# Attention inputs loaded in 1 KB runs, transposed by VectorE straight into place, and a new order for the first units

## The chip, the cores and the metric

The kernel runs on one core of a Trainium2 chip. The metric is the device time of one execution in microseconds (us). A run at a lower TensorE clock, or over 1.5% above the fastest of the same kernel, is marked slow and is not used in ratios. Several chips were used (the medians of the kernel before were 301.31 to 302.19 us), so each experiment is compared with the kernel before, timed in the same rounds.

In this kernel TensorE (PE in the profile) multiplies matrices, ScalarE (ACT) computes exponentials and copies, VectorE (DVE) does element-wise work and 32x32 block transposes, GpSimd is POOL, and SyncE (SP) issues most transfers (DMA; 129 of 197 issues in the profile before). SBUF is the on-chip memory, PSUM holds the products of TensorE. KB is 1024 bytes.

## The reference

Windowed attention with 8 global keys and a linear bias per head, then a layer of 8 experts in which every expert takes exactly 384 tokens, chosen greedily in order of the logits:

```python
# q, k, v: [4, 8, 768, 64] float32 (batch, heads, positions, head dimension)
scores = q @ k.T / 8 - slope[head] * dist    # keep: local (96 back) or global (first 8)
a = softmax(where(keep, scores, -1e9))
x = (a @ v) as [3072 tokens, 512]
logits = x @ w_gate                          # [3072, 8]
# greedy: largest logit first, 384 tokens per expert, each token once
out[tokens of e] = relu(x[tokens of e] @ w1[e]) @ w2[e]
```

## The kernel before

The attention runs in 8 units, u = 0 to 7; a unit is 4 heads of one batch element. The matmuls of the scores take queries and keys with the head dimension on the partitions (32 x 128 and 32 x 215 in the trace), while they lie in memory with the position outside. So a unit's 4 heads of q (768 KB) are loaded with 32 partitions for each head and 24 consecutive positions (6 KB) in each partition; VectorE transposes blocks of 32 x 32, and ScalarE copies the result into the order that the matmuls want.

```python
NJ = S_ // 32                       # 24 positions in a partition
qr = natp.tile([128, NJ, D_], FP32)
kr = natp.tile([128, NJ, D_], FP32)     # one buffer each: the load of unit u+2's keys
...                                     # waits for the transposes of unit u+1's
def load_u(u, dst, src):                # ONE transfer of 128 partitions x 6 KB
    b, hf = divmod(u, 2)
    nc.sync.dma_start(dst.rearrange("p j d -> p (j d)"),
                      src[b, 4*hf : 4*hf+4].rearrange("a (c j) d -> (a c) (j d)", j=NJ))

def blocks(key, src, g):                # writes 32 neighbouring floats at a time
    t = ttp.tile([128, NJ, 32], FP32, tag="tT", name=f"tT_{key}_{g}")
    nc.vector.transpose(out=t, in_=src[:, :, 32*g : 32*g+32])
    tTs[key, g] = t

def qT_out(u, g):                       # ScalarE puts the positions in order
    ...
    nc.scalar.copy(out=qTs[u][:, g, :].rearrange("p (c j) -> p c j", j=NJ),
                   in_=tTs.pop((f"q{u}", g)).rearrange("p j c -> p c j"))
...                                     # kA_out: the same for keys, in three copies
```

The program is written by hand in the order in which each engine meets its work. A unit's loop body (scores are made for unit `u` while unit `u-1` is attended, that is, its softmax weights are multiplied with v):

```python
load_u(0, kr, k); load_u(0, qr, q)
... # transposes and copies of unit 0
load_u(1, kr, k); load_u(1, qr, q)
... # w_gate
for n in range(NB): load_v(n)           # values of pairs 0 to 3, 20 transfers in 256-byte pieces
for u in range(NU + 1):
    ps = scores(u, 0); expo(u, 0, ps)   # TensorE, then exponentials on ScalarE
    if u == 0: build_W(0..3)            # mask tiles, ScalarE
    ... # u > 0: kT(u+1) on VectorE, load_u(u+2, kr, k), then masks of group 0
    av(A); oT_out(A, 0); oT_out(A, 1)   # attend of the first head pair of u-1
    pr = sums(A)                        # row sums and logits into a PSUM buffer
    ... # kA_out(u+1), qT(u+1, 0), qT_out(u+1, 0)
    sums_out(A, pr)                     # VectorE frees pr (transpose LT<-pr)
    ps = scores(u, 1); expo(u, 1, ps)
    if u == 0: build_W(4..7)
    ... # qT(u+1, 1), load_u(u+2, qr, q), masks of group 1
    ... # tok(A): TensorE transposes into PSUM (pk); tok_out(A): VectorE reads it (x)
    av(Bp); ...                         # attend of the second head pair
    ps = scores(u, 2); expo(u, 2, ps); mask(2*u, 2)
    pr = sums(Bp); sums_out(Bp, pr); ...
...
fill(4)                                 # four dummy matmuls before the routing
```

`pr` and `pk` share two PSUM buffers, so TensorE waits when VectorE comes late to empty them (11.46 us in the profile after).

The softmax here doesn't subtract the row's maximum and nothing guards it: scores larger than these inputs give would overflow.

Of the kernel before, what the change touches and what calls it, by code (L numbers as in the profile page):

```python
# [9 lines left out]
FP32 = mybir.dt.float32  # L10
# [7 lines left out]
B_, H_, S_, D_ = 4, 8, 768, 64  # L18
# [24 lines left out]
def kernel(  # L43
# [159 lines left out]
    with ExitStack() as actx:  # L203
# [24 lines left out]
        ttp = actx.enter_context(tc.tile_pool(name="ttp", bufs=2))  # L228
# [11 lines left out]
        NJ = S_ // 32  # L240
        qr = natp.tile([128, NJ, D_], FP32)
        kr = natp.tile([128, NJ, D_], FP32)
        kAs = [natp.tile([128, 2, NT, 128], FP32, name=f"kA{i}") for i in range(2)]
        NC5 = KT // NJ
        v7s = [natp.tile([128, 2, NT, D_], FP32, name=f"v7_{i}") for i in range(NB)]
        qTs = {}
        tTs = {}
        LASTK = S_ - KT * (NT - 1)

        def load_u(u, dst, src):  # L250
            b, hf = divmod(u, 2)
            nc.sync.dma_start(dst.rearrange("p j d -> p (j d)"),
                              src[b, 4 * hf : 4 * hf + 4].rearrange("a (c j) d -> (a c) (j d)", j=NJ))

# [12 lines left out]
        def blocks(key, src, g):  # L267
            t = ttp.tile([128, NJ, 32], FP32, tag="tT", name=f"tT_{key}_{g}")
            nc.vector.transpose(out=t, in_=src[:, :, 32 * g : 32 * g + 32])  # L269
            tTs[key, g] = t  # L270

        def kT(u, g):
            blocks(f"k{u}", kr, g)

        def kA_out(u, g):
            t = tTs.pop((f"k{u}", g)).rearrange("p j c -> p c j")
            kA = kAs[u % 2][:, g]
            n6 = NT - 1
            nc.scalar.copy(out=kA[:, 0:n6, 8:128].rearrange("p i (c j) -> p i c j", j=NJ),  # L279
                           in_=t[:, 0 : n6 * NC5, :].rearrange("p (i c) j -> p i c j", c=NC5))  # L280
            nc.scalar.copy(out=kA[:, n6, 8 : 8 + LASTK].rearrange("p (c j) -> p c j", j=NJ),
                           in_=t[:, n6 * NC5 : 32, :])
            nc.scalar.copy(out=kA[:, :, 0:8],
                           in_=t[:, 0:1, 0:8].to_broadcast([128, NT, 8]))

        def qT(u, g):
            blocks(f"q{u}", qr, g)

        def qT_out(u, g):
            if g == 0:  # L290
                qTs[u] = ktp.tile([128, 2, S_], FP32, tag="qT", name=f"qT{u}")
            nc.scalar.copy(out=qTs[u][:, g, :].rearrange("p (c j) -> p c j", j=NJ),  # L292
                           in_=tTs.pop((f"q{u}", g)).rearrange("p j c -> p c j"))
# [158 lines left out]
        with tc.manual_schedule():  # L452
# [6 lines left out]
            for g in range(2):  # L459
                kT(0, g)  # L460
                kA_out(0, g)
            for g in range(2):
                qT(0, g)
                qT_out(0, g)
# [8 lines left out]
            for u in range(NU + 1):  # L473
                A, Bp = 2 * (u - 1), 2 * (u - 1) + 1
                cur, prev, nxt = u < NU, u > 0, u + 1 < NU
                if cur:
                    ps = scores(u, 0)
                    expo(u, 0, ps)
                    if u == 0:
                        for h in range(4):  # L480
                            build_W(h)

                def keys():
                    if nxt:
                        kT(u + 1, 0)
                        kT(u + 1, 1)
                        if u + 2 < NU:
                            load_u(u + 2, kr, k)

                def first_masks():  # L490
                    if cur:
                        mask(2 * u, 0)
                        mask(2 * u + 1, 0)

                if u == 0:
                    first_masks()
                    keys()
                else:
                    keys()
                    first_masks()  # L500
                if prev:
                    av(A)
# [485 lines left out]
```

## Time and profile before

| | before |
|---|---|
| time, median of 3 runs | 302.26 us (301.77 to 302.31) |
| the profiled run | 304.70 us, span 302.9 us, clock 0.977 |
| start, to the first attend | 0 to 36.5 us |
| units 2 to 6, from scores to scores | 16.24 to 16.45 us each |
| unit 2's scores start | 51.06 us |
| last transposes to first routing matmul | 157.43 to 163.24 us |

The profiled run was 2.4 us slower than the median of the timed ones (its clock fell to 0.57 at 200 to 204 us, at the start of the experts).

Busy times on the profile's page (us, share of the span, instructions), then the start and one unit in the windows view. The columns of a window are its limits and length, busy time and count of PE, PEld, DVE, ACT and POOL, the granted clock (1.00 is TensorE's full speed), the mean busy share of the DMA engines (above 1 in places, 1.05 at 12 to 30 us) and GB/s:

```profile
PE 261.4 (86%) x3174; PEld 180.1 (59%) x3174; DVE 156.4 (52%) x301; ACT 143.8 (47%) x225; POOL 81.2 (27%) x126
```

```profile
0.00:36.00 36.00, 15.41 (x142) 12.53 (x144) 14.93 (x22) 23.67 (x31) 9.18 (x34) 1.00 0.84 218
...
51.06:67.30 16.24, 16.21 (x309) 13.70 (x308) 13.02 (x21) 12.95 (x18) 0.00 (x0) 1.00 0.72 177
```

In the units TensorE is busy for 16.21 of 16.24 us, so only TensorE's own work or a new wait changes them. In the start it is busy for less than half (15.41 of 36 us).

TensorE in the start, in the timeline (start, length, what, and the idle time before with its releaser):

```profile
11.31 1.10 PE L317 MATMUL ps<-qT,kA 32*128 32x215 f32 x8 [11.31 <-ACT qT L292]
...
16.22 4.01 PE L317 MATMUL ps<-qT,kA 32*128 32x215 f32 x32 [0.97 <-ACT P L331]
27.18 4.42 PE L317 MATMUL ps<-qT,kA 32*128 32x215 f32 x48 [6.94 <-ACT P L331]
32.65 3.94 PE L317 MATMUL ps<-qT,kA 32*128 32x215 f32 x32 [1.06 <-ACT P L331]
36.53 2.52 PE L365 MATMUL po<-P,v 128*64 128x215 f32 x36
```

The gap of 6.94 us is an exponential that stands on ScalarE behind mask tiles and copies of unit 1. The groups of instructions that the change touches (count, busy us, mean ns; then idle time before them):

```profile
L269 DVE STREAM_TRANSPOSE tT_q<-qr 128x768 f32<-128x768 f32 x16 | 15.6, 977 | 7.8 <-ACT kA L283 7.8
L269 DVE STREAM_TRANSPOSE tT_k<-kr 128x768 f32<-128x768 f32 x16 | 14.7, 954 | 4.6 <-DMA kr<-in_k_dram 4.6
L279 ACT COPY kA<-tT_k 128x720 f32<-128x720 f32 x16 | 23.7, 1484 | 6.3 <-DVE tT_k L269 6.3
L292 ACT COPY qT<-tT_q 128x768 f32<-128x768 f32 x16 | 24.8, 1556 | 0.0
```

Unit 2's keys are the next thing needed after the start. Their load is issued at 30.00 us, and VectorE begins to transpose them almost without a wait:

```profile
30.00 1.56 SPq L252 DMA_DIRECT2D kr<-in_k_dram  x1
...
35.74 1.84 DVE L269 STREAM_TRANSPOSE tT_k<-kr 128x768 f32<-128x768 f32 x2 [1.08 <-DMA kr<-in_k_dram]
```

### The profile page before, as it was taken

The page shows a single profiled execution, that of the slowest core. Times are in us where ns is not written, and L with a number is a line of the kernel's source. Part 1 is how long each engine was busy: PE and PEld are TensorE (multiplying, and loading weights), DVE is VectorE, ACT ScalarE, POOL GpSimd, SP SyncE. Part 2 cuts the span into 40 slices and gives each one's busy share as a digit, 9 for nine tenths or more (in the row PEclk, how much of TensorE's full clock was granted, in tenths as well). Part 3 has the DMA queues.
Part 4 walks back from the last instruction along what each step waited for, and adds up shares of the span by engine and source line. Part 5 has one row for each costly group of instructions (what it writes and reads, how often), then busy time and mean ns, then how long its engine had stood idle before and what let it go on. Part 6 is the DMA issues. An engine that isn't in the chain of part 4 may idle for free. (4 is left out here: it accounts for less than half of the span.)

```text
span 302.9 us, 7456 instructions
## 1 busy us (share of the span) xinstructions
PE 261.4 (86%) x3174; PEld 180.1 (59%) x3174; DVE 156.4 (52%) x301; ACT 143.8 (47%) x225; POOL 81.2 (27%) x126
## 2 busy tenths in 40 slices
PE   0454899999999999999997888879999998999940
PEld 0343788888888788888874343345655554555510
DVE  3255558879797978685524756322233222233020
ACT  3679686978869595963310000013522522513500
POOL 5060000003069000000004000473765556551230
PEclk9999999999999999999997999979999999999995
DMA  5799665695999998222024996159999999530220
GB/s 208 222 194 209 226 174 150 181 199 87 291 153 285 235 255 224 61 58 54 5 52 77 212 210 110 35 117 206 221 212 254 233 267 265 209 111 32 102 108 5
DMA packets 52568, 49.27 MB, mean 163 GB/s; under 512 B 29744, under 2 KB 44080, under 8 KB 52528
## 3 DMA queue, kind: packets, MB, share of 16 engines
q0 software_dynamic: 15680, 26.22, 41.4%
q1 hardware_dynamic: 36848, 22.50, 28.1%
q8 instruction: 27, 0.44, 0.6%
q14 instruction: 13, 0.11, 0.1%
HBM read 56.05 MB, written 9.44 MB: 216 GB/s over the span
## 5 line engine op out<-in xcount | busy, mean ns | idle before, releaser
L317 PE MATMUL ps<-qT,kA 32*128 32x215 f32 (+2 forms) x896 | 54.2, 369 | 20.6 <-ACT qT L292 11.6
L928 ACT ACTIVATE hT<-ph 128x384 bf16<-128x384 f32 x64 | 31.4, 491 | 71.9 <-PE ph L925 71.3
L317 PEld LDWEIGHTS ps<-qT,kA 32*128 32x128 f32 x896 | 45.4, 207 | 27.2 <-ACT qT L292 12.2
L331 ACT ACTIVATE P<-ps 128x860 f32<-128x860 f32 (+1 forms) x48 | 41.0, 893 | 27.5 <-PE ps L317 26.8
L345 DVE TENSOR_TENSOR P<-P,Wm 128x860 f32<-128x860 f32 (+1 forms) x32 | 32.9, 1049 | 18.0 <-ACT P L331 10.5
L365 PE MATMUL po<-P,v 128*64 128x215 f32 (+6 forms) x576 | 40.4, 292 | 0.0
L365 PEld LDWEIGHTS po<-P,v 128*64 128x64 f32 x576 | 34.4, 136 | 7.6 <-issue 3.5
L894 POOL DMA_INDIRECT xe<-x_tok,idi x24 | 23.4, 974 | 36.4 <-DVE idi L748 28.2
L934 PE MATMUL po<-w_late,hT 128*128 128x512 bf16 x144 | 32.9, 379 | 0.0
L937 DVE COPY ot<-po 128x512 f32<-128x512 f32 x24 | 16.5, 692 | 30.7 <-PE po L934 24.2
L925 PE MATMUL ph<-xT,w_late 128*128 128x384 bf16 x192 | 32.2, 326 | 0.0
L938 POOL DMA_INDIRECT out_dram<-ot,idi x24 | 23.6, 982 | 31.7 <-DVE ot L937 28.5
L934 PEld LDWEIGHTS <-hT 128*128 128x128 bf16 x192 | 18.3, 98 | 19.5
L576 POOL DMA_DIRECT2D w_late<-in_moe_w_dram x12 | 10.4, 874 | 69.1 <-DVE x L437 62.6
L907 DVE COPY xT<-pxe 128x512 bf16<-128x512 bf16 x24 | 9.5, 422 | 37.4 <-PE pxe L906 36.4
L396 PE MATMUL pr<-P,onesx 128*32 128x192 f32 (+11 forms) x768 | 27.6, 259 | 0.0
L279 ACT COPY kA<-tT_k 128x720 f32<-128x720 f32 x16 | 23.7, 1484 | 6.3 <-DVE tT_k L269 6.3
L925 PEld LDWEIGHTS <-w_late 128*128 128x128 bf16 x192 | 18.8, 98 | 13.1
L396 PEld LDWEIGHTS pr<-P,onesx 128*32 128x32 f32 x768 | 24.7, 109 | 2.1
L292 ACT COPY qT<-tT_q 128x768 f32<-128x768 f32 x16 | 24.8, 1556 | 0.0
L617 PE MATMUL pw<-w_early,ident_bf 128*128 128x512 bf16 x51 | 19.8, 389 | 2.7 <-DVE x L437 0.6
L338 DVE TENSOR_TENSOR P<-P,Wm 128x860 f32<-128x860 f32 x16 | 16.3, 1064 | 10.2 <-ACT P L331 10.2
(139 smaller groups left out, 263.5 us busy)
## 6 DMA issues: line engine op xcount, KB each, us to landing
w_late<-in_moe_w_dram POOLq DMA_DIRECT2D x12, 1024.0 KB, 12.5
kr<-in_k_dram SPq DMA_DIRECT2D x8, 768.0 KB
qr<-in_q_dram SPq DMA_DIRECT2D x8, 768.0 KB
v<-in_v_dram SPq DMA_DIRECT2D x32, 180.0 KB
w_early<-in_moe_w_dram POOLq DMA_DIRECT2D x8, 512.0 KB, 8.9
x_tok<-x SPq DMA_DIRECT2D x32, 96.0 KB
v<-in_v_dram SPq DMA_DIRECT2D x32, 14.0 KB
v<-in_v_dram SPq DMA_DIRECT2D x16, 24.0 KB
```

The lines of the kernel that those rows point to most:

```text
L279: nc.scalar.copy(out=kA[:, 0:n6, 8:128].rearrange("p i (c j) -> p i c j", j=NJ), in_=t[:, 0 : n6 * NC5, :].rearrange("p (i c) j -> p i c j ...
L292: nc.scalar.copy(out=qTs[u][:, g, :].rearrange("p (c j) -> p c j", j=NJ), in_=tTs.pop((f"q{u}", g)).rearrange("p j c -> p c j"))
L317: nc.tensor.matmul(ps[a // 2][:, a % 2, o : o + w], lhsT=kA[r, gd, i, :], rhs=qTt[r, gd, KT * i : KT * i + w], start=(gd == 0), stop=(gd = ...
L331: nc.scalar.activation(P[:, :, 0 : GW[g]], ps[w_][:, :, 0 : GW[g]], AF.Exp, scale=0.125)
L345: nc.vector.tensor_tensor(out=P[:, :, 0 : GW[g]], in0=P[:, :, 0 : GW[g]], in1=Wm[:, h0 : h0 + 2, lo : lo + GW[g]], op=ALU.mult)
L365: nc.tensor.matmul(po[n][bk][64 * t : 64 * t + 64, a - QB * bk : z - QB * bk], lhsT=v7[:, t, i, :], rhs=P[:, t, o + a - q0 : o + z - q0], ...
L396: nc.tensor.matmul(o_, lhsT=l_, rhs=r_, start=first[gq], stop=True, skip_group_check=True)
L894: tc.keep_in_program_order(nc.gpsimd.indirect_dma_start(out=xe, out_offset=None, in_=x_tok[:, :], in_offset=bass.IndirectOffsetOnAxis(ap=i ...
L925: nc.tensor.matmul(ph, lhsT=w1_of(e)[:, kc, 128 * fc : 128 * fc + 128], rhs=xT_e[:, kc, :, :].rearrange("p t n -> p (t n)"), start=(kc == ...
L928: nc.scalar.activation(hT[:, fc, :], ph, AF.Relu)
L934: nc.tensor.matmul(po, lhsT=hT[:, fc, 128 * t : 128 * t + 128], rhs=w2_of(e)[:, fc, :], start=(fc == 0), stop=(fc == NFC - 1))
L938: s = nc.gpsimd.indirect_dma_start(out=out[:, :], out_offset=bass.IndirectOffsetOnAxis(ap=idi[:, TSLAB * e + t : TSLAB * e + t + 1], axis= ...
```

## The change

The change has three parts.

1. **Layout.** The positions go to partitions four at a time (`NS = 4`, 1 KB runs), so that the transpose can write q into its final place, and k in position order, with a stride of four floats. ScalarE's copies of q go away, and those of k become contiguous. Each load becomes four transfers of 32 partitions.
2. **Order.** Unit 0's three score groups follow each other; its masks come later, and unit 1's loads and transposes are spread between them.
3. The four dummy matmuls before the routing are dropped.

```diff
-        NJ = S_ // 32
-        qr = natp.tile([128, NJ, D_], FP32)        # kr alike
+        NS = 4
+        qr = natp.tile([128, NBLK, NS, D_], FP32)  # kr alike; NBLK = 6
+        kTn = natp.tile([128, 2, S_], FP32)
         def load_u(u, dst, src):
             b, hf = divmod(u, 2)
-            nc.sync.dma_start(dst.rearrange("p j d -> p (j d)"),
-                              src[b, 4 * hf : 4 * hf + 4].rearrange("a (c j) d -> (a c) (j d)", j=NJ))
+            for a in range(4):
+                nc.sync.dma_start(dst[32 * a : 32 * a + 32].rearrange("c j s d -> c j (s d)"),
+                                  src[b, 4 * hf + a].rearrange("(j c s) d -> c j (s d)", j=NBLK, s=NS))
+        def blocks(dst, src, g):
+            nc.vector.transpose(out=dst.rearrange("p (j c s) -> p j s c", j=NBLK, s=NS),
+                                in_=src[:, :, :, 32 * g : 32 * g + 32])
... # kT writes kTn; kA_out copies kTn in three contiguous pieces; qT writes qTs[u]; qT_out is gone
-            for u in range(NU + 1):                # u == 0 leaves the loop:
+            ps = scores(0, 0); expo(0, 0, ps)      # (one statement a line in the kernel)
+            build_W(0); build_W(1)
+            kT(1); load_u(2, kr, k); weight_piece()
+            ps = scores(0, 1); expo(0, 1, ps)
+            kA_out(1); mask(0, 0); qT(1); load_u(2, qr, q)
+            ps = scores(0, 2); expo(0, 2, ps)
+            build_W(2); build_W(3)
+            ... # the other masks of unit 0
+            for u in range(1, NU + 1):
...
-            fill(4)
```

More of the change, by code (lines that the diff above doesn't have):

```diff
@@ L227 @@
         ktp = actx.enter_context(tc.tile_pool(name="ktp", bufs=2))
-        ttp = actx.enter_context(tc.tile_pool(name="ttp", bufs=2))
         tp = actx.enter_context(tc.tile_pool(name="tp", bufs=3))
@@ L239 @@
         NB = 4
-        NJ = S_ // 32
-        qr = natp.tile([128, NJ, D_], FP32)
-        kr = natp.tile([128, NJ, D_], FP32)
+        NS = 4
+        qr = natp.tile([128, NBLK, NS, D_], FP32)
+        kr = natp.tile([128, NBLK, NS, D_], FP32)
+        kTn = natp.tile([128, 2, S_], FP32)
         kAs = [natp.tile([128, 2, NT, 128], FP32, name=f"kA{i}") for i in range(2)]
-        NC5 = KT // NJ
         v7s = [natp.tile([128, 2, NT, D_], FP32, name=f"v7_{i}") for i in range(NB)]
         qTs = {}
-        tTs = {}
         LASTK = S_ - KT * (NT - 1)
@@ L265, in load_v, with kT, kA_out, qT @@
                               v[b, h : h + 2, KT * (NT - 1) : S_].rearrange("t u d -> u t d"))
-        def blocks(key, src, g):
-            t = ttp.tile([128, NJ, 32], FP32, tag="tT", name=f"tT_{key}_{g}")
-            nc.vector.transpose(out=t, in_=src[:, :, 32 * g : 32 * g + 32])
-            tTs[key, g] = t
-        def kT(u, g):
-            blocks(f"k{u}", kr, g)
-        def kA_out(u, g):
-            t = tTs.pop((f"k{u}", g)).rearrange("p j c -> p c j")
-            kA = kAs[u % 2][:, g]
-            n6 = NT - 1
-            nc.scalar.copy(out=kA[:, 0:n6, 8:128].rearrange("p i (c j) -> p i c j", j=NJ),
-                           in_=t[:, 0 : n6 * NC5, :].rearrange("p (i c) j -> p i c j", c=NC5))
-            nc.scalar.copy(out=kA[:, n6, 8 : 8 + LASTK].rearrange("p (c j) -> p c j", j=NJ),
-                           in_=t[:, n6 * NC5 : 32, :])
-            nc.scalar.copy(out=kA[:, :, 0:8],
-                           in_=t[:, 0:1, 0:8].to_broadcast([128, NT, 8]))
-        def qT(u, g):
-            blocks(f"q{u}", qr, g)
-        def qT_out(u, g):
-            if g == 0:
-                qTs[u] = ktp.tile([128, 2, S_], FP32, tag="qT", name=f"qT{u}")
-            nc.scalar.copy(out=qTs[u][:, g, :].rearrange("p (c j) -> p c j", j=NJ),
-                           in_=tTs.pop((f"q{u}", g)).rearrange("p j c -> p c j"))
+        def blocks(dst, src, g):
+            nc.vector.transpose(out=dst.rearrange("p (j c s) -> p j s c", j=NBLK, s=NS),
+                                in_=src[:, :, :, 32 * g : 32 * g + 32])
+        def kT(u):
+            for g in range(2):
+                blocks(kTn[:, g, :], kr, g)
+        def kA_out(u):
+            n6 = NT - 1
+            kA = kAs[u % 2]
+            nc.scalar.copy(out=kA[:, :, 0:n6, 8:128], in_=kTn[:, :, 0 : n6 * KT].rearrange("p g (i k) -> p g i k", i=n6))
+            nc.scalar.copy(out=kA[:, :, n6, 8 : 8 + LASTK], in_=kTn[:, :, n6 * KT : S_])
+            nc.scalar.copy(out=kA[:, :, :, 0:8],
+                           in_=kTn[:, :, 0:8].rearrange("p g (o k) -> p g o k", o=1).to_broadcast([128, 2, NT, 8]))
+        def qT(u):
+            qTs[u] = ktp.tile([128, 2, S_], FP32, tag="qT", name=f"qT{u}")
+            for g in range(2):
+                blocks(qTs[u][:, g, :], qr, g)
         wpieces = []
@@ L458 @@
                 nc.vector.memset(v7s[i][:, :, NT - 1, :], 0.0)
-            for g in range(2):
-                kT(0, g)
-                kA_out(0, g)
-            for g in range(2):
-                qT(0, g)
-                qT_out(0, g)
+            kT(0)
+            kA_out(0)
+            qT(0)
             load_u(1, kr, k)
@@ L472 @@
                                         in0=wg_sb[64 * t : 64 * t + 64], scalar1=LSCALE, scalar2=None, op0=ALU.mult)
-            for u in range(NU + 1):
+            ps = scores(0, 0)
+            expo(0, 0, ps)
+            build_W(0)
+            build_W(1)
+            kT(1)
+            load_u(2, kr, k)
+            weight_piece()
+            ps = scores(0, 1)
+            expo(0, 1, ps)
+            kA_out(1)
+            mask(0, 0)
+            qT(1)
+            load_u(2, qr, q)
+            ps = scores(0, 2)
+            expo(0, 2, ps)
+            build_W(2)
+            build_W(3)
+            mask(0, 1)
+            mask(0, 2)
+            for g in range(3):
+                mask(1, g)
+            for u in range(1, NU + 1):
                 A, Bp = 2 * (u - 1), 2 * (u - 1) + 1
-                cur, prev, nxt = u < NU, u > 0, u + 1 < NU
+                cur, nxt = u < NU, u + 1 < NU
                 if cur:
@@ L478 @@
                     expo(u, 0, ps)
-                    if u == 0:
-                        for h in range(4):
-                            build_W(h)
-                def keys():
-                    if nxt:
-                        kT(u + 1, 0)
-                        kT(u + 1, 1)
-                        if u + 2 < NU:
-                            load_u(u + 2, kr, k)
-                def first_masks():
-                    if cur:
-                        mask(2 * u, 0)
-                        mask(2 * u + 1, 0)
-                if u == 0:
-                    first_masks()
-                    keys()
-                else:
-                    keys()
-                    first_masks()
-                if prev:
-                    av(A)
-                    oT_out(A, 0)
-                    oT_out(A, 1)
-                    if A + NB < 2 * NU:
-                        load_v(A + NB)
-                    pr = sums(A)
-                if nxt:
-                    for g in range(2):
-                        kA_out(u + 1, g)
-                    qT(u + 1, 0)
-                    qT_out(u + 1, 0)
-                if prev:
-                    sums_out(A, pr)
+                    if u == 1:
+                        build_W(4)
+                        build_W(5)
+                if nxt:
+                    kT(u + 1)
+                    if u + 2 < NU:
+                        load_u(u + 2, kr, k)
+                if cur:
+                    mask(2 * u, 0)
+                    if u > 1:
+                        mask(2 * u + 1, 0)
+                av(A)
+                oT_out(A, 0)
+                oT_out(A, 1)
+                if A + NB < 2 * NU:
+                    load_v(A + NB)
+                pr = sums(A)
+                if nxt:
+                    kA_out(u + 1)
+                sums_out(A, pr)
                 weight_piece()
@@ L518 @@
                     expo(u, 1, ps)
-                    if u == 0:
-                        for h in range(4, 8):
-                            build_W(h)
+                    if u == 1:
+                        build_W(6)
+                        build_W(7)
                 if nxt:
-                    qT(u + 1, 1)
-                    qT_out(u + 1, 1)
+                    qT(u + 1)
                     if u + 2 < NU:
@@ L528 @@
                     mask(2 * u, 1)
+                    if u == 1:
+                        mask(2 * u + 1, 0)
                     mask(2 * u + 1, 1)
-                if prev and cur:
                     for hf in range(2):
@@ L533 @@
                         tok_out(A, hf, pk)
-                if prev:
-                    av(Bp)
-                    oT_out(Bp, 0)
-                    oT_out(Bp, 1)
-                    if Bp + NB < 2 * NU:
-                        load_v(Bp + NB)
+                av(Bp)
+                oT_out(Bp, 0)
+                oT_out(Bp, 1)
+                if Bp + NB < 2 * NU:
+                    load_v(Bp + NB)
                 if cur:
@@ L543 @@
                     mask(2 * u, 2)
-                if prev:
-                    pr = sums(Bp)
-                    sums_out(Bp, pr)
+                pr = sums(Bp)
+                sums_out(Bp, pr)
                 if cur:
                     mask(2 * u + 1, 2)
-                if prev:
-                    if not cur:
-                        for hf in range(2):
-                            pk = tok(A, hf)
-                            tok_out(A, hf, pk)
-                    for hf in range(2):
-                        pk = tok(Bp, hf)
-                        tok_out(Bp, hf, pk)
+                else:
+                    for hf in range(2):
+                        pk = tok(A, hf)
+                        tok_out(A, hf, pk)
+                for hf in range(2):
+                    pk = tok(Bp, hf)
+                    tok_out(Bp, hf, pk)
                 for _ in range(3):
-                    if u > 0 and late:
+                    if late:
                         late.pop(0)()
```

## The prediction

It was made from the profile before, the two kernels and a listing of how the change moves instructions on each engine. It counts units from 0, as this document does.

> **What bounds it now.** The windows view splits the span into a start (0 to 36 us), seven attention units of 16.2 to 16.5 us (36 to 153), an attention tail to 161.5, routing, and experts to 293.
>
> - Start: TensorE is busy 15.4 of 36 us, ScalarE 23.7. The timeline shows score groups at 11.3, 16.2, 27.2 and 32.7; the first attend starts at 36.5. The 7 us gap before 27.2 waits for two exponentials that stand on ScalarE behind four 0.74 us mask builds and unit 1's key and query copies (6 us). The DMA share is 0.8 to 1.2 from 12 to 30 us.
> - Units: TensorE is busy 16.21 of 16.24 us; ScalarE 13.0, VectorE 13.0 to 14.2. TensorE binds.
> - Routing is a latency chain; experts are TensorE-bound (106 of 113 us).
>
> **What changes, costed.** ScalarE loses per unit two query copies (1.556 us) and shortens the key copies (2 x (1.48+0.27+0.29)) to three contiguous ones: estimate 2.2 us, at the 1.03 ns per element of the 860-wide exponential. So 7.2 to 2.2 us per unit. The 720-element copy now costs 2.06 ns per element; it reads at a 128-byte stride. [...] VectorE's 384-element logit reduce with 32-byte stride takes 0.84 us against 0.35 us for 192 contiguous.
>
> The transposes move that stride to VectorE writes of exactly 16 bytes. No trace line shows such a write. I expect about 1.0 us (now 0.95 to 0.98), with 30% chance of 1.6 to 1.8 us, which would put VectorE at 16 to 17 us per unit, level with TensorE.
>
> q/k loads become four DMAs of 32 partitions in 1 KB runs: three more issues of 0.33 to 0.4 us each on SyncE; the first q and k, now landed by 6.2 us at 350 to 380 GB/s, should take to about 6.5 (k) and 9 (q).
>
> **Critical path.**
> 1. First scores stay at 11 to 12 us (later loads, shorter copies).
> 2. Score groups then follow at about 16, 21 and 26 us; first attend at 27 to 30 instead of 36.5.
> 3. Most of that is given back: unit 2's keys, queued behind the 256-byte v loads in a saturated DMA, land at about 36 us as now (VectorE waits for them today). VectorE meets that transpose before the row-sum transpose, which frees a PSUM buffer that TensorE needs. Estimate: unit 2's scores start at 48 to 49 instead of 51.06, gain 2.5 us.
> 4. Units: the third score group runs 2.23 us when its exponential was late, 1.96 when not; gain 0.25 us in five units, 1.4 us in all.
> 5. Four dummy matmuls ahead of routing (161.56, 1.88 us) stand before the first routing matmul at 163.24: gain 1.9 us.
> 6. Everything behind shifts by the sum, 5.8 us.
>
> **Prediction:** 296.0 us, 8 in 10 between 290.5 and 301.5. Faster by over 2%: 0.54; within 2%: 0.43; slower: 0.03.
>
> **What would show it.** Query copies gone, ScalarE about 40 us less busy over the span; transposes near 1.0 us; unit windows at 16.0 us; first attend at 27 to 30 with a wait of VectorE on unit 2's key load just after; no TensorE fill between attention and routing; expert stage unchanged in length.
>
> **What would make it wrong.** Strided transpose writes at half rate (near 302). Unit 2's keys landing well before 36, so that nothing is given back (near 291). The 32-partition DMAs [...] so that first scores slip to 13 or later. TensorE staying slow (32 matmuls in 4.0 us at first, 1.74 later) through all first score groups.

The two marked cuts are statements about the memory that no trace of this case shows. 2.5 + 1.4 + 1.9 = 5.8 us, set against the 302 us before. Both durations for the new transposes, about 1.0 us and 1.6 to 1.8 us, and the half rate at the end were estimates; the profile before has no such write to show them.

## The result, and the profile after

The changed kernel took 306.77 us (median of 4 runs, 305.90 to 307.13), the kernel before 302.19 us (4 runs). The ratio is 1.015, with a 95% interval of 1.0125 to 1.0175. Ratios here and below are the mean time of one kernel's fast runs over that of the other's fast runs of the same rounds, so they are not quite the ratio of the medians. The change costs 1.5%: within 2%, but on the other side of what was predicted, and outside the predicted range.

The same lines in the profile after (305.4 us span, clock 0.962). Busy times and windows; 55.03 and 71.06 are the starts of unit 2's and unit 3's scores:

```profile
PE 254.9 (83%) x3162; PEld 174.9 (57%) x3170; DVE 173.1 (57%) x301; ACT 108.1 (35%) x185; POOL 85.3 (28%) x126
```

```profile
0.00:36.00 36.00, 18.95 (x271) 14.86 (x271) 18.86 (x21) 15.85 (x23) 9.54 (x34) 1.00 0.96 188
...
38.00:44.00 6.00, 0.00 (x0) 0.00 (x0) 3.62 (x3) 0.64 (x1) 0.00 (x0) 0.50 0.69 142
...
55.03:71.06 16.03, 16.00 (x309) 13.41 (x309) 15.23 (x21) 8.67 (x13) 0.00 (x0) 1.00 0.90 173
71.06:88.35 17.29, 16.21 (x310) 13.39 (x309) 16.32 (x25) 8.56 (x13) 1.98 (x7) 1.00 0.99 165
```

ScalarE lost 35.7 us, as meant. VectorE gained 16.7 us and is now about as busy in a unit as TensorE. The DMA engines are busier (0.96 of the start's time) and move less (188 GB/s instead of 218). TensorE in the start:

```profile
11.33 1.10 PE L309 MATMUL ps<-qT,kA 32*128 32x215 f32 x8 [11.33 <-DVE qT L267]
...
16.10 3.80 PE L309 MATMUL ps<-qT,kA 32*128 32x215 f32 x32 [0.97 <-ACT P L323]
20.42 2.72 PE L309 MATMUL ps<-qT,kA 32*128 32x215 f32 x48 [0.52 <-ACT P L323]
23.94 2.50 PE L309 MATMUL ps<-qT,kA 32*128 32x215 f32 x32 [0.80 <-ACT P L323]
26.38 2.52 PE L357 MATMUL po<-P,v 128*64 128x215 f32 x36
...
32.48 0.55 PE L421 MATMUL pk<-ident,oT 128*128 128x128 f32 x3
44.49 0.90 PE L421 MATMUL pk<-ident,oT 128*128 128x128 f32 x3 [11.46 <-DVE LT L401]
45.32 4.73 PE L357 MATMUL po<-P,v 128*64 128x215 f32 x36
```

The start does what it was meant to do: the first attend begins 10.15 us earlier. Then TensorE stands for 11.46 us, waiting for VectorE to empty a PSUM buffer (`LT<-pr`). In that time the clock falls to half (0.50 at 38 to 44 us), and the next attend, with 36 matmuls as before, takes 4.73 us instead of 2.52. What held VectorE is unit 2's keys, issued 3.92 us later than before and 4.64 us later in VectorE's hands. Of the 3.92 us, 3.13 were there when the first v was issued (14.86 us, before 11.73): v stands behind unit 1's queries, whose load waited for slower transposes and took 1.76 us to issue instead of 0.33.

```profile
33.92 1.77 SPq L251 DMA_DIRECT2D kr<-in_k_dram  x4
...
40.38 2.89 DVE L267 STREAM_TRANSPOSE kTn<-kr 128x768 f32<-128x768 f32 x2 [11.43 <-DMA kr<-in_k_dram]
```

The groups show the other cost: a transpose takes 1.59 to 1.60 us instead of 0.95 to 0.98.

```profile
L267 DVE STREAM_TRANSPOSE kTn<-kr 128x768 f32<-128x768 f32 x16 | 24.1, 1588 | 18.8 <-DMA kr<-in_k_dram 18.8
L267 DVE STREAM_TRANSPOSE qT<-qr 128x768 f32<-128x768 f32 x16 | 24.2, 1603 | 0.8 <-DMA qr<-in_q_dram 0.8
L277 ACT COPY kA<-kTn 128x1440 f32<-128x1440 f32 x8 | 11.1, 1393 | 25.9 <-DVE kTn L267 25.9
```

And in the long unit the row sums wait for a buffer that VectorE had not yet read:

```profile
85.31 1.63 PE L388 MATMUL pr<-P,onesx 128*32 128x192 f32 x45 [0.96 <-DVE x L429]
```

The ledger, after minus before, from the starts in the two timelines:

| | before | after | difference |
|---|---|---|---|
| first attend | 36.53 | 26.38 | -10.15 |
| unit 2's scores | 51.06 | 55.03 | +3.97 |
| unit 7's scores | 132.60 | 139.51 | +6.91 |
| first routing matmul | 163.24 | 168.59 | +5.35 |
| first token gather | 192.91 | 197.57 | +4.66 |
| end of the profiled span | 302.9 | 305.4 | +2.5 |
| timed medians | 302.19 | 306.77 | +4.58 |

The profiled spans differ by less than the medians because the profiled run of the kernel before lost 2.2 us after the token gather; its clock was 0.57 at 200 to 204 us, that of the changed kernel 1.00. Up to there the trace's difference (4.66) is that of the medians (4.58).

So the lost time is in two places: before unit 2 (14.1 us from the first attend to there) and in units 2 to 6 (2.9 us more). The units took 16.03, 17.29, 16.61, 17.11 and 17.44 us; before, 16.24 to 16.45.

### The profile page after: what moved, and what is told of

It is laid out like the page before. It is cut to its first block, busy times and chain, and to the rows that moved or that the text cites. A ratio compares the mean times of both kernels' runs of the same rounds, so it can differ in the third digit from the quotient of the medians.

```text
span 305.4 us, 7474 instructions
## 1 busy us (share of the span) xinstructions
PE 254.9 (83%) x3162; PEld 174.9 (57%) x3170; DVE 173.1 (57%) x301; ACT 108.1 (35%) x185; POOL 85.3 (28%) x126
## 5 line engine op out<-in xcount | busy, mean ns | idle before, releaser
L309 PE MATMUL ps<-qT,kA 32*128 32x215 f32 (+2 forms) x896 | 48.7, 351 | 14.1 <-DVE qT L267 11.5
L309 PEld LDWEIGHTS ps<-qT,kA 32*128 32x128 f32 x896 | 40.6, 195 | 20.3 <-ACT kA L279 11.3
L357 PE MATMUL po<-P,v 128*64 128x215 f32 (+6 forms) x576 | 42.6, 302 | 0.0
L357 PEld LDWEIGHTS po<-P,v 128*64 128x64 f32 x576 | 36.0, 142 | 8.2 <-issue 3.4
L267 DVE STREAM_TRANSPOSE kTn<-kr 128x768 f32<-128x768 f32 x16 | 24.1, 1588 | 18.8 <-DMA kr<-in_k_dram 18.8
L925 PE MATMUL po<-w_late,hT 128*128 128x512 bf16 x138 | 31.7, 379 | 0.1
L421 PE MATMUL pk<-ident,oT 128*128 128x128 f32 x96 | 16.9, 294 | 13.2 <-DVE LT L401 11.5
L267 DVE STREAM_TRANSPOSE qT<-qr 128x768 f32<-128x768 f32 x16 | 24.2, 1603 | 0.8 <-DMA qr<-in_q_dram 0.8
L421 PEld LDWEIGHTS pk<-ident,oT 128*128 128x128 f32 x96 | 10.2, 143 | 20.4 <-DVE LT L401 14.7
```

The costliest lines, as they stand in the source:

```text
L267: nc.vector.transpose(out=dst.rearrange("p (j c s) -> p j s c", j=NBLK, s=NS), in_=src[:, :, :, 32 * g : 32 * g + 32])
L309: nc.tensor.matmul(ps[a // 2][:, a % 2, o : o + w], lhsT=kA[r, gd, i, :], rhs=qTt[r, gd, KT * i : KT * i + w], start=(gd == 0), stop=(gd = ...
L357: nc.tensor.matmul(po[n][bk][64 * t : 64 * t + 64, a - QB * bk : z - QB * bk], lhsT=v7[:, t, i, :], rhs=P[:, t, o + a - q0 : o + z - q0], ...
L421: nc.tensor.transpose(pk[:, bb, :], oTs[n][:, 3 * hf + bb].rearrange("c g r -> c (g r)"), ident)
L925: nc.tensor.matmul(po, lhsT=hT[:, fc, 128 * t : 128 * t + 128], rhs=w2_of(e)[:, fc, :], start=(fc == 0), stop=(fc == NFC - 1))
```

## The experiments

Theories that remained after this reading:

- **W, strided writes.** The transposes are slow because of the write stride. This makes units long and frees `kr` later.
- **L, loads.** The new loads are slower than the old ones, and unit 2's keys come late for that reason.
- **O, order.** The new order itself is at fault: it only moves the wait, because unit 2's keys stand behind the 20 transfers of v.

Seventeen kernels were run; all were correct. Units are counted from 0; where a text says "second unit's keys" or "third unit's scores", e9, e13 and e14 mean unit 2, while "the second unit" in e12 is unit 1. Cuts marked in the texts of e5, e7 and e9 are reasons that no trace here shows.

### e1: the order alone

The changed kernel with the old tiles, loads, transposes and copies (so: part 2 and part 3 of the change).

```diff
-            for a in range(4):                      # new loads, new tiles
-                nc.sync.dma_start(dst[32 * a : 32 * a + 32]..., ...)
+            nc.sync.dma_start(dst.rearrange("p j d -> p (j d)"), ...)   # as before
-            nc.vector.transpose(out=dst.rearrange("p (j c s) -> p j s c", ...), ...)
+            nc.vector.transpose(out=t, ...)         # as before, with ScalarE's copies
```

> The changed order and no dummy matmuls, but the old 6 KB loads, contiguous transposes and ScalarE copies. Layout theory (strided transpose writes plus slow 1 KB loads cost the time, the order is sound): block transposes at 0.95 to 0.98 us, unit 2's keys there at 35 to 37 us, unit 2's scores at 48 to 50 us (51.06 before, 55.03 changed), units at 16.0 to 16.3 us, time 297 to 300 us. Rival (the new order itself starves something): unit 2's scores at 53 us or later, time 303 us or more.

Measured: 299.08 us (297.56 to 300.59), ratio 0.9898 (0.9825 to 0.9970). Transposes 0.96 and 0.97 us. First attend at 31.96, unit 2's keys at 35.26, unit 2's scores at 49.98, units of 16.2 us but for one of 16.83.

```profile
35.26 1.84 DVE L269 STREAM_TRANSPOSE tT_k<-kr 128x768 f32<-128x768 f32 x2 [2.02 <-DMA kr<-in_k_dram]
```

The order is not at fault; with the dummy matmuls gone it gains 1%. O falls as an explanation of the loss, though part of it comes back in e4.

### e2: the layout alone

The kernel before, in its old order and with its dummy matmuls, with the new tiles, loads, transposes and copies.

```diff
-            nc.sync.dma_start(dst.rearrange("p j d -> p (j d)"), ...)
+            for a in range(4):
+                nc.sync.dma_start(dst[32 * a : 32 * a + 32]..., ...)
-            nc.vector.transpose(out=t, ...); nc.scalar.copy(out=qTs[u]...)
+            nc.vector.transpose(out=qTs[u]...rearrange("p (j c s) -> p j s c", ...), ...)
```

> The old order and the dummy matmuls, with the new loads, strided transposes and contiguous key copies. Layout theory: transposes 1.60 us, unit 2's keys at 38 to 41 us, units 2 to 6 at 16.6 to 17.4 us, time 307 to 311 us. Rival (order): units as before at 16.2 to 16.4 us, time 301 to 303 us.

Measured: 315.98 us (313.21 to 317.18), ratio 1.0488 (1.0426 to 1.0550). Transposes 1.57 and 1.59 us, unit 2's keys at 40.32, unit 2's scores at 56.14, units from 16.33 to 17.74. The time is 5 us above the 307 to 311, which is not explained. The layout is the whole loss. It costs 4.9% in the old order. In the new one it costs 2.5% (1.015 over 0.990), about half as much.

### e3: old loads, and in-place writes with a wider stride

With the old 6 KB runs a transpose in place must write floats 96 bytes apart.

```diff
+        NJ = S_ // 32
+            nc.sync.dma_start(dst.rearrange("p j d -> p (j d)"), ...)       # as before
-            nc.vector.transpose(out=dst.rearrange("p (j c s) -> p j s c", j=NBLK, s=NS), ...)
+            nc.vector.transpose(out=dst.rearrange("p (c j) -> p j c", j=NJ), ...)
```

> The changed kernel with the old 6 KB loads; the transposes still write queries and keys in place, now with a 96-byte stride. If the 1 KB loads delay unit 2's keys: keys at 35 to 37 us instead of 40.4, and unit 2's scores at 50 to 52 us, time 302 to 304 us if a 96-byte stride writes as slowly as a 16-byte one (1.6 us). If the loads are not the cause of the late keys: keys at 39 us or later, time 306 us or more. If the write rate gets worse with the stride: transposes well above 1.6 us and units above 17.5 us.

Measured: 318.62 us (315.10 to 319.52), ratio 1.0523 (1.0436 to 1.0611).

```profile
L266 DVE STREAM_TRANSPOSE qT<-qr 128x768 f32<-128x768 f32 x16 | 31.9, 2101 | 0.0
```

A transpose takes 2.10 us, the units 18.37 to 20.60 us. The loads are the old ones here, so the write stride alone sets the transposes' time and makes units long. Unit 2's keys came at 37.74, between the two cases, since slow transposes also free the buffer later (the second load of keys was issued at 9.28 us, before at 7.22; unit 2's at 33.11, in e1 at 30.63).

### e4: the changed kernel with half of v later

```diff
-            for n in range(NB):
+            for n in range(2):
                 load_v(n)
...
             load_u(2, qr, q)
+            for n in range(2, NB):
+                load_v(n)
             ps = scores(0, 2)
```

> The changed kernel with the v loads of pairs 2 and 3 issued after unit 2's keys and queries. Queue theory (the keys are late because they stand behind v loads that nobody needs yet): unit 2's keys land at 28 to 32 us, VectorE's 11.4 us wait shrinks below 3 us, TensorE stays warm, unit 2's scores at 45 to 48 us, time 297 to 300 us. Rival (all loads of the start are bound by the DMA rate, so what is moved back is waited for elsewhere): another wait of 5 us or more for v appears, time 303 us or more.

Measured: 301.37 us (299.36 to 303.73), ratio 0.9993 (0.9908 to 1.0079). Unit 2's keys were issued at 21.10 instead of 33.92 and transposed at 34.79 instead of 40.38; unit 2's scores began at 48.75, 6.28 us earlier than in the changed kernel. The keys came later than the text had them: their transfer, side by side with v's, still took 13.7 us from issue to use. So VectorE still waited 3.94 us, and TensorE did not stay warm: after a gap of 2.56 us the clock was 0.50 at 40 to 43 us (0.63 in the mean of 38.92 to 43.50) and the attend took 4.17 us. Scores and time missed their ranges too, by 0.75 and 1.4 us.

```profile
34.79 2.92 DVE L267 STREAM_TRANSPOSE kTn<-kr 128x768 f32<-128x768 f32 x2 [3.94 <-DMA kr<-in_k_dram]
...
38.92 0.55 PE L421 MATMUL pk<-ident,oT 128*128 128x128 f32 x3 [2.56 <-DVE LT L401]
39.40 4.17 PE L357 MATMUL po<-P,v 128*64 128x215 f32 x36
```

The units stayed long (16.03, 17.28, 16.63, 17.90, 16.40). This separates the two losses: the wait before unit 2 was the keys, and with most of it gone W's share is left.

### e5: the order with the loads in four parts

Run e1 with four transfers of 32 partitions, and nothing else: still 6 KB runs and contiguous writes.

```diff
-            nc.sync.dma_start(dst.rearrange("p j d -> p (j d)"), ...)
+            for a in range(4):
+                nc.sync.dma_start(dst[32 * a : 32 * a + 32].rearrange("p j d -> p (j d)"),
+                                  src[b, 4 * hf + a].rearrange("(c j) d -> c (j d)", j=NJ))
```

> Experiment e1 (new order, old layout) with each q/k load split in four DMAs of 32 partitions, rows still 6 KB. If the split in 32 partitions makes the new loads slow[...]: 220 to 270 GB/s at 2 to 6 us as in the changed kernel, first q later than 8.5 us, unit 2's keys at 37 us or later (35.3 in e1). If only the 1 KB runs do: 340 to 390 GB/s, first q before 7.5 us, keys at 35 to 36 us, time within 1 us of e1's 299.1.

Measured: 305.28 us (303.45 to 306.18), ratio 1.0136 (1.0075 to 1.0196). 240 GB/s at 4 to 6 us where e1 has 390; unit 2's keys at 38.59, its scores at 52.37. Later, VectorE waited 3.66 us for unit 6's queries, and unit 5, from scores to scores, took 18.44 us (16.83 in e1):

```profile
38.59 1.84 DVE L270 STREAM_TRANSPOSE tT_k<-kr 128x768 f32<-128x768 f32 x2 [4.19 <-DMA kr<-in_k_dram]
...
111.97 1.84 DVE L270 STREAM_TRANSPOSE tT_q<-qr 128x768 f32<-128x768 f32 x2 [3.66 <-DMA qr<-in_q_dram]
```

Splitting the load by itself costs 2.4% against e1's ratio, without any slow transpose. L holds.

### e6: the order with 1 KB pieces over all partitions

Run e1 with six transfers of 128 partitions x 1 KB.

```diff
-            nc.sync.dma_start(dst.rearrange("p j d -> p (j d)"), ...)
+            for j0 in range(0, NJ, 4):
+                nc.sync.dma_start(dst[:, j0 : j0 + 4, :]..., rows[:, j0 : j0 + 4, :]...)
```

> Experiment e1 with each q/k load cut in six DMAs of 128 partitions and 1 KB per partition; the layout in memory is the old one. If 1 KB runs make the new loads slow: 220 to 270 GB/s at 2 to 6 us and unit 2's keys at 37 us or later. If the split over partitions does: 330 GB/s or more, keys at 35 to 36 us, time within 1 us of e1.

Measured: 303.00 us (299.85 to 304.05), ratio 1.0045 (0.9954 to 1.0137). 264 GB/s at 4 to 6 us, unit 2's keys at 40.11. SyncE needs 2.78 us to issue the six, which by itself would hold a load at 283 GB/s (an estimate: 768 KB over the 2.78 us). So this run did not tell partitions from pieces; e9, e13, e16 and e17 were made for it.

### e7: half the stride

The changed kernel with `NS = 2`: 512-byte runs, and writes 8 bytes apart.

```diff
-        NS = 4
+        NS = 2
... # 12 blocks of positions instead of 6 in both rearrangements
```

> The changed kernel with 2 tokens per run: 512-byte loads, transpose writes at a stride of 8 bytes[...]. [...] transposes at 1.0 us (1.60 at 16 bytes), units at 16.0 to 16.1 us, no wait of the row sums' matmuls for VectorE; the loads get slower, so unit 2's keys land at 41 us or later and the time is 303 to 308 us. If any stride costs the same: transposes at 1.6 us and units at 16.6 to 17.4 us.

Measured: 308.67 us (305.41 to 312.70; the three fast runs 305.41 to 309.27), ratio 1.0221 (1.0138 to 1.0304). Its profiled run fell in the slow state (clock 0.935), so only single durations are read from it; e14 repeats the layout in a fast run. The transposes are back at 0.96 us, as in the first of the two cases (the second is that any stride costs the same). The time is not better: unit 2's keys still come at 39.80, and e14 shows a second cause.

### e8, e11: the order, with half of v later

Run e1 with e4's edit, first in 3 rounds, then once more in 5.

> Experiment e1 (new order, old loads, transposes and copies) with the v loads of pairs 2 and 3 behind unit 2's keys and queries, as in e4. Expected the best so far: keys at 28 to 33 us, unit 2's scores at 46.5 to 48.5 us (49.98 in e1), time 295.5 to 298 us. If the whole start is bound by the DMA rate and v is missed instead: 298.5 us or more.

> Run e8 again beside e12, in more rounds. Expected: 295.5 to 298 us, ratio 0.983 to 0.990 to before.

Measured: e8 296.59 us (294.96 to 298.81), ratio 0.9861 (0.9779 to 0.9942); e11 296.63 us (295.74 to 297.29), ratio 0.9825 (0.9790 to 0.9860). Unit 2's keys are issued at 17.64 us in e8, and VectorE meets them without any wait:

```profile
33.21 1.83 DVE L269 STREAM_TRANSPOSE tT_k<-kr 128x768 f32<-128x768 f32 x2
```

Unit 2's scores begin at 48.12. This version beats the kernel before by 1.4 to 1.8%, and so the changed kernel, at 1.5% the other way, by about 3%.

### e9: the four loads in another order of heads

Run e5 with `for a in (0, 2, 1, 3)`, so that two transfers in a row do not go to neighbouring partitions.

> Run e5 (each 768 KB load of queries or keys as four transfers of 32 partitions) with the heads loaded in the order 0, 2, 1, 3, so that two transfers that follow each other do not go to neighbouring partitions. Theory[...]: at least 330 GB/s at 2 to 6 us as in e1 (341 and 390), first query transpose before 7.5 us, second unit's keys at 35 to 36.5 us, time 299 to 302. Rival (it is the number of transfers, or their small size, whatever the partitions): 240 GB/s as in e5, first query transpose at 9.5 us, keys at 38.5 us, time 304 to 306.

Measured: 301.67 us (300.66 to 303.84), ratio 1.0028 (0.9978 to 1.0079). The rate at the start missed the expectation: 230 GB/s at 2 to 4 us and 261 at 4 to 6. But unit 2's keys came at 37.45, and in the units the DMA engines were less busy (0.80 against 0.88 in e5). The ratio is 1.1% below e5's.

### e13, e16, e17: how many transfers, and how large the pieces

Run e1 with the load as four transfers of 128 partitions x 1.5 KB (e13), as one transfer in pieces of 1.5 KB, which 256 free bytes in the destination keep apart (e16), and as two transfers of 128 partitions x 3 KB (e17).

```diff
-            nc.sync.dma_start(dst.rearrange("p j d -> p (j d)"), ...)
+            for j0 in range(0, NJ, 6):              # e13; e17 has 12 for 6
+                nc.sync.dma_start(dst[:, j0 : j0 + 6, :]..., rows[:, j0 : j0 + 6, :]...)
+            nc.sync.dma_start(dst[:, :, 0 : 6, :].rearrange("p n j d -> p n (j d)"), ...)   # e16
```

> Run e1 with each 768 KB load as four transfers of all 128 partitions x 1.5 KB: as many transfers as e5, and of the same 192 KB each. Theory (what slows e5 is that a transfer covers only 32 partitions): 330 GB/s or more at 2 to 6 us, share of the DMA engines' time at 42 to 150 us 0.68 to 0.72 as in e1 and e6, second unit's keys at 35.3 to 37 us, time 299 to 301. Rival (it is the number and the size of the transfers): about 240 GB/s, share 0.85 to 0.9, keys at 38.5 us, time 304 to 306. Between the two: both contribute.

> Run e1 with each 768 KB load still one transfer of 128 partitions, but in pieces of 1.5 KB (256 bytes are left free between them in the destination). If the number of transfers slows e13: 340 to 390 GB/s at 2 to 6 us, unit 2's keys (counted from 0) transposed from 35.0 to 35.8 us as in e1, time 298 to 300.5. If the size of the pieces does: 270 to 280 GB/s, unit 2's keys at 37.5 to 38 us, time 301 to 303.

> Run e1 with each 768 KB load as two transfers of 128 partitions x 3 KB. If each further transfer costs a fixed time (e13's three further ones made unit 2's keys 2.59 us later): about 0.9 us later than e1, so 36.1, and 330 to 350 GB/s at 4 to 6 us. If the size of the pieces alone counts: between e1 and e13, depending on e16; as e1 if e16 is.

Measured: e13 301.81 us (300.68 to 303.63), ratio 1.0009 (0.9960 to 1.0059); e16 299.78 us (298.16 to 300.38), ratio 0.9915 (0.9854 to 0.9976); e17 298.86 us (297.50 to 300.00), ratio 0.9897 (0.9831 to 0.9962).

The seven kernels with the new order and contiguous writes, with before and after for comparison. Keys: when the transpose of unit 2's keys begins.

| run | transfers x partitions | piece | GB/s at 2 to 6 us | DMA share 42 to 150 us | keys, us | ratio |
|---|---|---|---|---|---|---|
| before | 1 x 128 | 6 KB | 366 | 0.69 | 35.74 | 1 |
| e1 | 1 x 128 | 6 KB | 366 | 0.68 | 35.26 | 0.9898 |
| e16 | 1 x 128 | 1.5 KB | 316 | 0.71 | 36.54 | 0.9915 |
| e17 | 2 x 128 | 3 KB | 316 | 0.70 | 34.79 | 0.9897 |
| e13 | 4 x 128 | 1.5 KB | 273 | 0.71 | 37.85 | 1.0009 |
| e6 | 6 x 128 | 1 KB | 260 | 0.72 | 40.11 | 1.0045 |
| e9 | 4 x 32, heads 0 2 1 3 | 6 KB | 246 | 0.80 | 37.45 | 1.0028 |
| e5 | 4 x 32 | 6 KB | 241 | 0.88 | 38.59 | 1.0136 |
| after | 4 x 32 | 1 KB | 247 | 0.91 | 40.38 | 1.0150 |

The windows at 42 to 150 us of e1, e5, e9 and e13, in this order:

```profile
42.00:150.00 108.00, 104.89 (x1990) 87.84 (x1982) 84.79 (x136) 77.97 (x109) 14.71 (x32) 0.98 0.68 158
```

```profile
42.00:150.00 108.00, 102.50 (x1979) 86.38 (x1978) 84.38 (x134) 80.02 (x113) 14.76 (x32) 1.00 0.88 167
```

```profile
42.00:150.00 108.00, 104.91 (x1995) 88.11 (x1992) 85.46 (x136) 79.68 (x111) 14.77 (x32) 0.98 0.80 166
```

```profile
42.00:150.00 108.00, 104.00 (x2014) 87.64 (x2012) 86.52 (x138) 79.71 (x113) 14.75 (x32) 1.00 0.71 165
```

Two effects are apart here. Transfers that cover 32 partitions keep the DMA engines busy for longer at about the same bytes per second (0.88 at 167 GB/s against 0.71 at 165); transfers over all partitions do not, down to the smallest pieces run (1 KB in e6, 0.72 at 169 GB/s). And the rate at the start falls both with more transfers and with smaller pieces: 366 GB/s with one in 6 KB pieces, 316 with one in 1.5 KB pieces and with two of 3 KB, 241 to 273 with four or six. (e16 moved 234 at 2 to 4 us and 397 at 4 to 6, so the later window alone would hide it.) How late unit 2's keys come is not explained so simply: e17's two transfers cost nothing, against the 0.9 us, and e16's small pieces cost 1.28 us, which neither case had (its issue takes 0.55 us instead of 0.36). Of e5's delay of 3.33 us, e13 has 2.59 without any small span of partitions, but its pieces are small too. Whether a transfer has a fixed cost, and which, is therefore not settled; that splitting in four and narrow spans cost is.

### e10: the kernel before without the dummy matmuls

```diff
-            fill(4)
```

> The kernel before without the four dummy matrix products ahead of the routing, and nothing else. Theory (they delay the first routing product by their own 1.9 us less the wait they cover): first routing product 1.5 to 1.9 us sooner after the last transposes than in before (5.81 us there), time 0.5 to 0.6% shorter. Rival (they keep the clock up, so that what they cost comes back later): no change in time, within 0.2%.

Measured: 301.71 us (299.52 to 303.02), ratio 0.9990 (0.9945 to 1.0034). In the traces, before has the dummies in front of the first routing matmul:

```profile
157.43 1.12 PE L429 MATMUL pk<-ident,oT 128*128 128x128 f32 x6
...
161.56 1.88 PE L617 MATMUL pw<-w_early,ident_bf 128*128 128x512 bf16 x4 [0.65 <-DVE x L437]
163.24 1.06 PE L642 MATMUL pk<-ident,Lb 128*128 128x128 f32 x4
```

and e10 does not:

```profile
158.28 1.12 PE L429 MATMUL pk<-ident,oT 128*128 128x128 f32 x6
...
162.51 0.68 PE L642 MATMUL pk<-ident,Lb 128*128 128x128 f32 x4 [0.74 <-DVE x L437]
```

From the last transposes to the first routing matmul it is 4.23 us instead of 5.81: 1.58 us sooner, as the theory had it. The times don't show it; the interval reaches from a gain of 0.55% to a loss of 0.34%, so neither the full 0.5% nor nothing is excluded.

### e12: the copies of unit 1's keys sooner

Run e8, with two mask tiles built after the copies of unit 1's keys instead of before.

```diff
-            build_W(0); build_W(1)
             kT(1); load_u(2, kr, k); weight_piece()
+            kA_out(1)
             ps = scores(0, 1); expo(0, 1, ps)
-            kA_out(1); mask(0, 0)
             qT(1)...
+            build_W(0); build_W(1); mask(0, 0)
```

> Run e8 with the key copies of the second unit right after the first exponential, and the building of two mask tiles after them. If ScalarE's copies between 24.5 and 27.3 us, which stood before the third exponential, set the start of the next scores: third unit's scores at about 47 us against 48.12, time 295.5 to 296.5. If the start is set by the keys' transposes or the first attend instead: no difference from e11 within 0.2%.

Measured: 296.35 us (295.02 to 297.80), ratio 0.9830 (0.9793 to 0.9867). Unit 2's scores came at 47.32 us, in e11 at 48.66. The trace moves by 1.34 us as expected; the ratio does not differ from e11's 0.9825, but 1.34 us is 0.45%, and the intervals do not exclude that.

### e14, e15: both repairs on the changed kernel

The changed kernel with 8-byte strides (e7) and with half of v later (e4); in e15 also with heads in the order 0, 2, 1, 3.

> The changed kernel with 512-byte runs (writes 8 bytes apart, as e7) and the loads of v2 and v3 behind the second unit's keys and queries (as e4). Theory (two causes, slow strided writes and keys that come late behind v): transposes 0.96 us, units 15.95 to 16.1 us, third unit's scores at 47 to 49 us (48.75 in e4), time 293.5 to 297, so level with or better than e8 (296.59). Rival (the slow loads of 32 partitions cost as much on their own): third unit's scores past 50 us, time 298 or more.

> Run e14 with the heads loaded in the order 0, 2, 1, 3 (as e9). In e9 that order left the start's rate as it was, and took the DMA share at 42 to 150 us from 0.88 to 0.80. Expected: same as e14 within 0.3%, unless a load is waited for in the units, in which case up to 1% faster.

Measured: e14 303.08 us (301.44 to 308.14; the four fast runs 301.44 to 303.16), ratio of the fast runs 1.0002 (0.9959 to 1.0045). In e15 five of six runs counted as slow, the profiled one among them, and one fast run took 298.42 us. In e14 most of what was expected of the trace was there: transposes of 0.96 us, unit 2's scores at 48.71, and four units of 15.96 or 15.97 us. Yet the fast runs missed by 4.4 us or more: unit 5 took 23.36 us. The groups show the fast transposes, the timeline one wait on VectorE:

```profile
L268 DVE STREAM_TRANSPOSE qT<-qr 128x768 f32<-128x768 f32 x16 | 14.7, 959 | 9.2 <-DMA qr<-in_q_dram 9.2
...
110.92 1.84 DVE L268 STREAM_TRANSPOSE qT<-qr 128x768 f32<-128x768 f32 x2 [6.56 <-DMA qr<-in_q_dram]
```

and behind it TensorE:

```profile
115.18 2.97 PE L389 MATMUL pr<-P,onesx 128*32 128x192 f32 x45 [5.60 <-DVE x L430]
```

A load of unit 6's queries, whose issue began at 99.28 us, was not in hand before 110.92 us. From 90 to 110 us, when GpSimd's weight loads run too, the DMA engines were at 1.19 and moved 214 GB/s; before moved 250 GB/s there at 1.12. The changed kernel moved 214 as well, at 1.16, and its load of these queries took as long: issued at 102.01, in hand at 113.62. There VectorE, with slow transposes, came to it late and waited only 0.19 us. e5, with 6 KB pieces in four transfers of 32 partitions, moved 215 GB/s in this stretch and has the same wait (3.66 us); e13, with four transfers over all partitions, moved 238 and has none, and e6, with six, has no long unit 5 (16.71 us, against 18.44 in e5). So in these traces narrow transfers are enough to bring the wait, and e14's fast transposes uncover it. How much its 512-byte pieces add is not shown. They come with the small stride: the layout has 64 bytes of run for each byte of stride, since a row of 64 floats is 256 bytes and the stride is 4 bytes per row.

## Why the prediction was wrong

The prediction was a sum of three terms: 2.5 us before unit 2's scores, 1.4 us in the units, 1.9 us before the routing, 5.8 us in all. Measured: -3.97, -2.94 and, in the trace, +1.57 us (5.81 to 4.24). Two terms had the wrong sign: the first is off by 6.5 us, the second by 4.3.

1. **First scores and the score groups: right, the last a little early.** 11.33 (predicted 11 to 12), then 16.10, 20.42 and 23.94 (predicted 16, 21, 26); first attend 26.38 (predicted 27 to 30).
2. **"Most of that is given back": right in mechanism, wrong in size.** The text named the wait itself: keys behind v in a busy DMA, VectorE met the transpose before `LT<-pr`, and TensorE stood for a PSUM buffer. The step that failed is "unit 2's keys ... land at about 36 us as now". They were in hand at 40.38. Two costs move them, and each was run alone: split loads give 38.59 (e5), slow transposes 37.74 (e3, at 2.10 us each), neither 35.26 (e1). Much of it is queueing: the keys were issued at 30.63 us in e1, 32.93 in e5, 33.11 in e3 and 33.92 in the changed kernel. The text feared narrow spans only for the first scores, and let the transfer of keys take as long as before.
3. **The cold clock was not in the sum.** After 11.46 us without work the granted clock was 0.50 (38 to 44 us) and the attend took 4.73 us instead of 2.52. How long a gap brings this is not shown: the clock was at 0.50 after 2.56 us in e4, and after 1.84 us in e1, but not after 1.84 us in e5 (the pages' slices there have 7 tenths in e1, at 44.8 to 52.3 us, and 9 in e5, at 45.5 to 53.1). The row sums that follow took 2.97 us in e1, the first line below, and 1.63 in e5, the second:

```profile
45.34 2.97 PE L409 MATMUL pr<-P,onesx 128*32 128x192 f32 x45 [1.84 <-DVE x L450]
...
48.63 1.63 PE L410 MATMUL pr<-P,onesx 128*32 128x192 f32 x45 [1.84 <-DVE x L451]
```

4. **"I expect about 1.0 us" for a transpose: wrong, it took 1.60.** The other case was in the text, with a chance of 30%, as "near 302"; it was 306.77, since the keys came late as well. e3, e7 and e14 settle that the write stride does it: 0.95 to 0.98 us at 4 bytes, 0.96 at 8, 1.57 to 1.60 at 16, 2.10 at 96. The time was the same at 4 and 8 bytes and grew beyond. (The reduces that the text compared, 0.84 us for 384 elements at a 32-byte stride and 0.35 for 192, are 2.2 and 1.8 ns per element, all of their time included: thin support for a price of strides.)
5. **"Unit windows at 16.0 us": wrong for four of five.** 16.03 came once. With 1.60 us transposes VectorE is busy for 15.2 to 16.3 us in a unit, and TensorE waited for `x` and `LT`. e14 has 15.96 us three times: the term was right in mechanism and hung on point 4. e4 has the long units with keys at 34.79, so points 2 and 4 are separate losses, though slow transposes have a share in both.
6. **Dummy matmuls: the size in the trace was right** (1.57 us of 1.9), and e10 has 1.58. Whether the time gains as much is not resolved.
7. **ScalarE -36 us against "about 40": right.** Its copies took 2.06 ns per element at a 128-byte read stride (1484 ns for 720) and 0.97 contiguous (1393 ns for 1440). It was off the critical path in the units, so it bought nothing there.

What remains open: whether a transfer has a fixed cost (e16 and e17 do not fit one number), why a write stride of 96 bytes costs more than one of 16 (2.10 against 1.60 us), how much the 512-byte pieces add to e14's wait for queries (6.56 us, against 3.66 in e5), why a gap of 1.84 us sometimes halves the clock and sometimes does not, and whether e12's 1.3 us are in the time (its noise would hide them).

The best kernel is the new order with the old layout and half of v behind unit 2's keys (e8, e11; e12 is as fast): 296.4 to 296.6 us.

## What to carry to other kernels

This layout saved copies on an engine that did not bind, and other engines paid for it. Count the write stride of the transpose (0.96 us at 8 bytes, 1.60 at 16), the partitions that one transfer spans (DMA share 0.88 with 32, 0.71 with 128, e5 and e13), and the number of transfers, each from a line of the profile or a small run, before counting the saved copies. When a start becomes faster, ask which load the next stage needs and what stands before it in the queue; here, moving the loads of two of the four first pairs of v behind the keys took the changed kernel's ratio from 1.015 to 0.999. And an idle stretch of TensorE can cost more than its length: after 11.46 us without work the next 36 matmuls took 4.73 us instead of 2.52. A wait can also hide behind a slower engine, as that for unit 6's queries did, and show only when that engine is mended.
